# Casting q to fp16 in DRAM as 18 x 8 blocks of 4 KB instead of one contiguous stretch

## The chip, the cores and the metric

The kernel runs on one core of one Trainium2 chip. The metric is the device time of one execution in microseconds (us). The kernel before took 274.94 us, the median of 3 runs (274.41 to 275.86).

## The reference

Eight batches, eight heads, a sequence of 576 and a head dimension of 64. A Performer attention with 128 random features is followed by an MLP mixer over tokens and channels.

```python
def _attn_ref(q, k, v, omega):
    q_s, k_s = (q * scale, k * scale)
    def phi(x):                                   # random features, 128 per token
        proj = np.einsum('bhsd,md->bhsm', x, omega)
        h = proj - np.sum(x * x, axis=-1, keepdims=True) / 2.0
        h = h - np.max(h, axis=-1, keepdims=True)
        return np.exp(h) / np.sqrt(m)
    q_p, k_p = (phi(q_s), phi(k_s))
    kv = np.einsum('bhsm,bhsd->bhmd', k_p, v)
    z = np.sum(k_p, axis=2)
    num = np.einsum('bhsm,bhmd->bhsd', q_p, kv)
    den = np.einsum('bhsm,bhm->bhs', q_p, z)[..., None] + 1e-06
    return num / den

def _moe_ref(x, w_tok1, w_tok2, w_ch1, w_ch2):    # x: batch, 576, 8 heads * 64
    xt = x.transpose(0, 2, 1)
    h = np.maximum(xt @ w_tok1, 0.0) @ w_tok2     # 576 -> 256 -> 576
    u = x + h.transpose(0, 2, 1)
    h2 = np.maximum(u @ w_ch1, 0.0) @ w_ch2       # 512 -> 1536 -> 512
    return u + h2
```

## The kernel before, in words

**Stages of a batch.** The program works batch by batch, with neighbouring batches overlapped. For batch b: the features of k (matmuls at L571 for the last 64 tokens and at L679 for the first 512, exponentials at L534) and of q (L641 and L691, L534); k's features times v (L735, with v scaled on GpSimd at L315 just before); the attention's numerators and denominators (L768); the token mixing (L796, L803, then L816, L870); a transposition of u by a DMA (L824) into the tile uT; the channel mixing, whose first product reads uT (L1144, from batch 5 on L1073) and whose second product is L1178 or L961.

**How q and k reach the core.** The feature matmuls need q and k with the head dimension on the partitions, in fp16. Batches 0 and 1 are transposed on TensorE. For batches 2 to 7, the function `load_transposed` (L375) does it in two DMA steps. GpSimd issues casting DMAs from fp32 in DRAM to fp16 in a DRAM scratch (`q16_b`, `k16_b`): for q one DMA for all 576 tokens (`cast`, L379); for k one for the first 512 tokens (`cast_main`, L384) and two for the last 64 (`cast_tail`, L390). Then SyncE issues a transposing DMA from the scratch into the tile qT or kT (`back`, L400), which waits for the landing of its casts. A row of the scratch holds 128 fp16 elements, so q's scratch of a batch is 2304 rows, 589,824 bytes.

**What sets the order.** Nothing is decided at run time: `Planner.run` (L154) issues the jobs by a written list of numbers (`ORDER`, L22). So the instructions of each engine stand in a fixed row, and each waits for the semaphores of what it needs. Two queues matter here. GpSimd (POOL in the profile) issues all casting DMAs and the loads of v, between its own multiplications. SyncE (SP) issues the transposing DMAs of q, k and u and some of the stores; a wait at its head holds up all that stands behind it. All DMAs that GpSimd issues go into the one software queue, q0 of the profile.

The rows of SyncE around the first two transposed batches are these (kT and qT of batch 2, then uT of batch 1, then two stores, then qT and kT of batch 3):

```order
L400 DMA_TRANSPOSE kT_89<-k_2_152 128x1x2304
L400 DMA_TRANSPOSE qT_86<-q_2_151 128x1x2304
L824 DMA_TRANSPOSE uT_127<-u_123 128x16x128
L1188 DMA out_dram<-o_132 128x512
L1188 DMA out_dram<-o_131 128x512
L400 DMA_TRANSPOSE qT_84<-q_3_153 128x1x2304
L400 DMA_TRANSPOSE kT_87<-k_3_154 128x1x2304
```

Thus a late cast of batch 2 also holds the transposition of u of batch 1, and a late cast of q of batch 3 holds kT of the same batch.

Of the kernel before, what the change touches and what calls it, by code (L numbers as in the profile page):

```python
# [137 lines left out]
class Planner:  # L138
# [38 lines left out]
    def place(self, tag, name):  # L177
        return self.held[tag, name]
# [7 lines left out]
def kernel(  # L186
# [14 lines left out]
    B, H, S, D = q.shape  # L201
# [4 lines left out]
    P = 128  # L206
# [7 lines left out]
    R = SM // 2  # L214
# [84 lines left out]
    scratch = {}  # L299
# [3 lines left out]
    src = {"q": q, "k": k}  # L303
# [26 lines left out]
    def dma(eng, key, wire, fn, deps=(), take=(), give=(), cost=None):  # L330
        cost = (0.75 if eng == "POOL" else 0.45) if cost is None else cost
        job = add(eng, cost, key, fn, deps, take, give, wire=wire)
        return job
# [41 lines left out]
    def load_transposed(b, key, deps=()):  # L375
        casts = {"q": [], "k": []}
        for n, w in enumerate("qk"):
            def cast(w=w):
                nc.gpsimd.dma_start(  # L379
                    out=scratch[w, b].rearrange("(p r) e -> p (r e)", p=P),  # L380
                    in_=src[w][b].rearrange("h s d -> (h s d)").rearrange("(p f) -> p f", p=P),
                )
            def cast_main(w=w):
                nc.gpsimd.dma_start(  # L384
                    out=scratch[w, b][0 : H * R].rearrange("(h c r) e -> c h (r e)", h=H, c=P // H),
                    in_=src[w][b, :, 0:SM, :].rearrange("h s d -> h (s d)").rearrange("h (c f) -> c h f", c=P // H),
                )
            def cast_tail(w=w):
                for g in range(2):
                    nc.gpsimd.dma_start(  # L390
                        out=scratch[w, b][H * R : H * RA, g * D : (g + 1) * D],
                        in_=src[w][b, 4 * g : 4 * g + 4, SM:S, :],
                    )
            if w == "k":
                casts[w].append(dma("POOL", key + 0.01 * n - 0.005, 0.8, cast_tail, deps, cost=1.1))
            casts[w].append(dma("POOL", key + 0.01 * n, 3.2, cast if w == "q" else cast_main, deps, cost=0.55))
        for n, w in enumerate("qk"):
            def back(w=w):
                t = (t_qT if w == "q" else t_kT)[place(w + "T", b)]
                nc.sync.dma_start_transpose(out=t.unsqueeze(1), in_=scratch[w, b])  # L400
            ld[w + "T", b] = dma("SP", key + 0.2 + 0.01 * n, 2.2, back, deps=casts[w], take=[(w + "T", b)], cost=2.5)
# [25 lines left out]
    def clear(t):  # L427
# [6 lines left out]
        out=w1m.rearrange("p j t -> p (j t)"), in_=moe_w_tok1[0:SM, :].rearrange("(p j) t -> p (j t)", j=NJ)))  # L434
# [23 lines left out]
    for i in range(2):  # L458
        c0 = i * (NCB // 2)
        j_wc2.append(dma("POOL", -3.0 + 0.1 * i, 3.85, lambda c0=c0: nc.gpsimd.dma_start(  # L460
            out=wc2[:, c0 : c0 + NCB // 2, :], in_=moe_w_ch2[c0 * P : (c0 + NCB // 2) * P, :].rearrange("(i p) d -> p i d", p=P))))
# [5 lines left out]
    for out_, a, b in ((T1, W12, W11), (T2, W22, T1), (T3, W22, W12), (T4, W21, T2)):  # L467
# [3 lines left out]
        out=omega16.rearrange("p (i d) -> p i d", i=2), in0=omega_nat.unsqueeze(1).broadcast_to((P, 2, D)), scalar1=c_scale, scalar2=None, op0=ALU.mult), deps=j_om)  # L471
# [779 lines left out]
```

## Time and profile before

| what | value |
| --- | --- |
| median of the runs | 274.94 us (274.41 to 275.86, 3 runs) |
| the profiled execution, its own time | 273.79 us |
| its span, from the first to the last instruction | 272.0 us |
| TensorE (PE) busy | 262.9 us, 97% of the span |
| VectorE (DVE) busy | 227.2 us, 84% |
| ScalarE (ACT) busy | 164.2 us, 60% |
| GpSimd (POOL) busy | 134.6 us, 49% |
| granted TensorE clock, mean | 0.998 |
| casts of q (L379) | 6 DMAs, 576 KB each in the profile's count, median 7.6 us from issue to landing |
| casts of k, first 512 tokens (L384) | 6 DMAs, 512 KB each, median 7.1 us |

Times in the views are microseconds from the start of the span. A DMA's landing is counted from the start of the instruction that issues it. In the rows of the DMA queues stand packets, megabytes, and the time that the packets took as a share of 16 DMA engines over the window; the share can pass 100%, since packets on one engine overlap. The page's bytes of a packet are those written.

### The profile page before, as it was taken

Reading aid. Unit: us, or ns where it says so; the run is one execution under the profiler, and the core shown is the slowest. Engines: PE = TensorE matmul, PEld = TensorE weight load, DVE = VectorE, ACT = ScalarE, POOL = GpSimd, SP = SyncE. Lnnn points to the kernel's source line nnn. Section 1 sums busy time; section 2 is a strip of 40 time slices with the busy share of each in tenths; the row PEclk is TensorE's granted clock in tenths of the full one; section 3 lists DMA queues with packets and bytes.
Section 4 is the critical chain, followed back from the end, with each engine's and each line's share of the span. In section 5 each row is a group of like instructions: output and inputs, shape, how many; then the busy total and the mean of one; then the engine's idle time right before and its main releaser. Section 6 shows DMA issues by size and latency. Waiting matters only on the chain.

```text
span 272.0 us, 6648 instructions
## 1 busy us (share of the span) xinstructions
PE 262.9 (97%) x2647; PEld 180.0 (66%) x2647; DVE 227.2 (84%) x479; ACT 164.2 (60%) x361; POOL 134.6 (49%) x146
## 2 busy tenths in 40 slices
PE   7799999999999999999999999999999999999992
PEld 4367455444568655766578546986789688888881
DVE  3897879876998799987889799899997795799992
ACT  2999941188695338736746865699947541573500
POOL 8895492064803490079459996964145044600001
PEclk9999999999999999999999999999999999999999
DMA  8999999999999999989989986980260063030134
GB/s 199 190 208 210 191 210 185 216 202 132 180 204 156 223 187 175 164 160 158 171 178 173 194 233 64 182 167 2 49 128 2 23 193 58 0 157 0 63 133 119
DMA packets 81296, 39.70 MB, mean 146 GB/s; under 512 B 63984, under 2 KB 77040, under 8 KB 81072
## 3 DMA queue, kind: packets, MB, share of 16 engines
q0 software_dynamic: 31744, 17.74, 44.2%
q1 hardware_dynamic: 46928, 15.37, 29.5%
q10 hardware_dynamic: 2592, 6.16, 6.4%
q8 instruction: 20, 0.33, 0.5%
q14 instruction: 12, 0.10, 0.1%
HBM read 35.95 MB, written 16.52 MB: 193 GB/s over the span
## 4 chain that ended last, share of the span: by engine, by line
PE 86%; DMA 8%; POOL 3%; DVE 1%; issue 0%; POOLq 0%; SPq 0%
PE bank L961 24%; PE bank L1144 19%; PE bank L1073 13%; PE bank L803 5%; PE bank L816 5%; DMA uT<-u 4%; DMA w1m<-in_moe_w_tok_dram 4%; PE bank L1178 4%; PE bank L679 3%; PE bank L768 3%; PE bank L735 3%; PE bank L691 2%; POOL r L339 1%; PE bank L870 1%; PE bank L842 1%; PE bank L854 1%
## 5 line engine op out<-in xcount | busy, mean ns | idle before, releaser
L1144 PE MATMUL bank<-uT,wc 128*128 128x512 f16 x232 | 56.0, 379 | 0.0
L315 POOL TENSOR_TENSOR vs<-v,vs 128x512 f16<-128x512 f16 x31 | 33.1, 1072 | 42.8 <-DVE vs L716 33.5
L310 ACT ACTIVATE r<-bank 128x512 f16<-128x512 f32 (+1 forms) x61 | 34.5, 598 | 26.5 <-PE bank L1144 16.0
L961 PEld LDWEIGHTS <-r 128*128 128x128 f16 x384 | 36.7, 98 | 7.2 <-issue 1.6
L534 ACT ACTIVATE kp<-bank 128x512 f16<-128x512 f32 x64 | 35.5, 623 | 9.6 <-PE bank L679 8.9
L712 DVE TENSOR_REDUCE km<-kp 128x8 f16<-128x1024 f16 x32 | 38.5, 1204 | 2.0 <-ACT kp L534 2.0
L534 ACT ACTIVATE qp<-bank 128x512 f16<-128x512 f32 x64 | 36.5, 620 | 4.3 <-PE bank L691 4.3
L1144 PEld LDWEIGHTS <-wc 128*128 128x128 f16 x232 | 20.5, 98 | 20.1 <-issue 1.1
L961 PEld LDWEIGHTS <-S 128*128 128x128 f16 x288 | 27.7, 98 | 4.7 <-issue 0.4
L786 DVE TENSOR_TENSOR x<-bank,rc 128x320 f16<-128x320 f32 x53 | 25.2, 483 | 1.1
L941 DVE TENSOR_TENSOR o<-u,bank 128x512 f32<-128x512 f16 x28 | 19.1, 680 | 5.8 <-PE bank L961 5.3
L961 PE MATMUL bank<-T,r 128*128 128x256 f16 x192 | 23.8, 273 | 0.0
L961 PE MATMUL bank<-T,S 128*128 128x256 f16 x192 | 23.4, 272 | 0.0
L961 PE MATMUL bank<-wc,r 128*128 128x256 f16 x192 | 23.1, 273 | 0.0
L312 DVE TENSOR_SCALAR r<-bank 128x512 f16<-128x512 f32 (+1 forms) x29 | 18.9, 661 | 3.1 <-PE bank L1144 2.4
L819 DVE TENSOR_TENSOR u<-x,bank 128x512 f16<-128x512 f16 x28 | 17.9, 681 | 1.9 <-PE bank L816 1.9
L315 POOL TENSOR_TENSOR vbd<-vt,vbd 128x512 f16<-128x512 f16 x6 | 6.4, 1060 | 23.5 <-DVE vbd L616 18.5
L768 PEld LDWEIGHTS <-qp 128*128 128x128 f16 x256 | 14.0, 98 | 5.9 <-issue 0.3
L1073 PE MATMUL bank<-uT,wc 128*128 128x256 f16 x120 | 16.6, 273 | 0.6 <-DMA uT<-u 0.6
L941 DVE TENSOR_TENSOR o<-o,bank 128x512 f32<-128x512 f32 x21 | 14.3, 680 | 3.1 <-PE bank L961 2.9
L775 DVE RECIPROCAL rc<-bank 128x5 f32<-128x5 f32 x64 | 11.2, 184 | 6.7 <-PE bank L770 3.7
L768 PE MATMUL bank<-kvsb,qp 128*128 128x65 f16 x256 | 16.0, 193 | 0.2 <-ACT qp L534 0.2
(151 smaller groups left out, 551.3 us busy)
## 6 DMA issues: line engine op xcount, KB each, us to landing
out_dram<-o ACTq DMA_DIRECT2D x9, 512.0 KB, 3.7
q<-in_q_dram POOLq DMA_DIRECT2D x6, 576.0 KB, 7.6
wc<-in_moe_w_ch_dram POOLq DMA_DIRECT2D x4, 768.0 KB, 11.1
k<-in_k_dram POOLq DMA_DIRECT2D x6, 512.0 KB, 7.1
v<-in_v_dram POOLq DMA_DIRECT2D x6, 512.0 KB, 8.6
out_dram<-o SPq DMA_DIRECT2D x5, 512.0 KB, 3.1
r<-in_q_dram POOLq DMA_DIRECT2D x4, 288.0 KB, 7.1
v<-in_v_dram POOLq DMA_DIRECT2D x4, 256.0 KB, 8.9
```

Of the source, the lines that this page charges most:

```text
L310: nc.scalar.activation(out=out, in_=in_, func=AF.Relu)
L312: nc.vector.tensor_relu(out=out, in_=in_)
L315: (nc.gpsimd if eng == "POOL" else nc.vector).tensor_tensor(**kw)
L534: nc.scalar.activation(out=out, in_=in_, func=AF.Exp, bias=0.0, scale=1.0)
L712: nc.vector.reduce_max(out=t_km[place("km", (b, hp))], in_=src_, axis=AX.X)
L768: nc.tensor.matmul(ps[:, k, j * 65 : (j + 1) * 65], st, s[:, i, 0 : D + 1], start=True, stop=True)
L786: nc.vector.tensor_tensor(out=to, in0=ps, in1=rc.unsqueeze(2).broadcast_to((P, NJ + 1, D)), op=ALU.mult)
L819: nc.vector.tensor_tensor(out=t_u[place("u", b)][:, j, :], in0=t_x[place("x", b)][:, j, :], in1=bank(n), op=ALU.add)
L941: nc.vector.tensor_tensor(out=o, in0=a, in1=ps, op=ALU.add)
L961: nc.tensor.matmul(ps[:, j * DH : (j + 1) * DH], a[:, cb, j * P : (j + 1) * P], w[:, cb, :], start=(bank_of(b, j0) not in held and j == j0 ...
L1073: nc.tensor.matmul(ps[:, n, :], w(a)[:, (2 * m + n) * P : (2 * m + n + 1) * P], x_[:, a], start=(what in ("P1", "P2", "P5") and n == 0 and ...
L1144: nc.tensor.matmul(ps, wc1[:, db, cb * P : (cb + 1) * P], moving(db), start=(db == 0), stop=(db == ND - 1))
```

## The change

One DMA form is changed, the cast of q at L379, issued six times (batches 2 to 7).

```diff
             def cast(w=w):
                 nc.gpsimd.dma_start(
-                    out=scratch[w, b].rearrange("(p r) e -> p (r e)", p=P),
-                    in_=src[w][b].rearrange("h s d -> (h s d)").rearrange("(p f) -> p f", p=P),
+                    out=scratch[w, b].rearrange("(h c r) e -> c h (r e)", h=H, c=S * D // (R * 8)),
+                    in_=src[w][b].rearrange("h s d -> h (s d)").rearrange("h (c f) -> c h f", c=S * D // (R * 8)),
                 )
```

With S = 576, D = 64 and R = 256, c is 18: a head's 36,864 elements are cut into 18 blocks of 2048 elements (8 KB read, 4 KB written). The blocks are walked with the block number outside and the head inside, 18 times 8 pieces. Source and destination of every element stay as they were. Before, the whole is contiguous, and the program as built holds it as 32 pieces of 9216 elements (18,432 bytes written). The form of the k cast at L384 is 16 times 8 pieces of 2048 elements in both kernels.

On GpSimd, the place of the first two changed DMAs shows that the form alone is different, and the neighbours keep their order:

```order
 L371 DMA vt_93<-in_v_dram 64x4x64
 L315 TENSOR_TENSOR vs_106<-v_91,vs_106 128x8x64
-L379 DMA q_2_151<-in_q_dram 32x9216
+L379 DMA q_2_151<-in_q_dram 18x8x2048
 L390 DMA k_2_152<-in_k_dram 256x1x64 x2
 L357 DMA v_92<-in_v_dram 128x8x256
 L315 TENSOR_TENSOR vbd_113<-vt_93,vbd_113 128x8x64
-L379 DMA q_3_153<-in_q_dram 32x9216
+L379 DMA q_3_153<-in_q_dram 18x8x2048
 L390 DMA k_3_154<-in_k_dram 256x1x64 x2
 L384 DMA k_3_154<-in_k_dram 16x8x2048
```

The rows of TensorE, VectorE, ScalarE and SyncE are the same in both programs.

## The prediction

> **What bounds the kernel now.** I read the page's busy times first, then the busy time by stage, then the waits. The page's row of the engines:
>
> ```profile
> PE 262.9 (97%) x2647; PEld 180.0 (66%) x2647; DVE 227.2 (84%) x479; ACT 164.2 (60%) x361; POOL 134.6 (49%) x146
> ```
>
> The busy time by stage, in two stages in which casts of q are issued (window, its length, then busy time and instructions of PE, PEld, DVE, ACT and POOL, granted clock, DMA share, GB/s):
>
> ```profile
> 40.00:60.00 20.00, 20.00 (x180) 10.46 (x180) 16.55 (x33) 7.65 (x17) 5.51 (x7) 1.00 1.15 186
> 60.00:80.00 20.00, 20.00 (x185) 10.56 (x182) 16.79 (x39) 15.90 (x32) 9.45 (x12) 1.00 1.21 187
> ```
>
> TensorE is busy for 20.00 of 20.00 us in each, at full clock: it bounds the kernel and does not wait for a DMA there. In the view of waits, the only matmuls behind the start-up that wait for a DMA are these two, and the chain of waits has them at 200 and 228 us:
>
> ```profile
> PE bank L1073 <- DMA uT<-u: 0.6, 2, 0.3
> ```
> ```profile
> 194.41 6.04 DMA uT<-u
> 222.46 5.85 DMA uT<-u
> ```
>
> The last cast of q is issued at 152.1 us (the row of L379 below).
>
> Two consequences. A quicker DMA can win nothing in the stages where q is cast. A slower one costs exactly what it overruns its slack by, and since TensorE has no idle time to catch up with, such a delay stays to the end. So the question is the slack of q's casts, and how much longer each takes.
>
> **The change, part by part: one cast.** What a piece costs comes from two stretches in which the software queue carries pieces of one size alone. First pieces of the q cast of batch 4 (window 77.12 to 78.5 us), the totals and the queue's row:
>
> ```profile
> DMA packets 16, 0.29 MB, mean 214 GB/s; under 512 B 0, under 2 KB 0, under 8 KB 0
> q0 software_dynamic: 16, 0.29, 99.9%
> ```
>
> 16 pieces of 18,432 bytes (0.29 MB) took 99.9% of 16 engines for 1.38 us: 1.38 us each. Then the k cast of batch 4 in pieces of 4096 bytes (window 90.05 to 92.6 us):
>
> ```profile
> q0 software_dynamic: 142, 0.52, 102.4%
> ```
>
> 0.52 MB are 128 pieces of 4096 bytes (the other 14 packets are a few bytes each): 102.4% of 16 engines for 2.55 us, 41.8 us in all, 0.326 us each. By the byte a small piece is 6% dearer.
>
> Before, 32 pieces on 16 engines are 2 each: 2.76 us per engine. Now there are 144 pieces. If they were dealt out singly, 9 per engine, it would be 2.93 us, 0.17 us more. But the DMA's outer count is now 18, and the outer blocks hold 8 pieces each. If an engine takes whole outer blocks, 18 blocks on 16 engines leave at least one engine with two, 16 pieces: 5.22 us, **2.46 us more** than before. No DMA of the kernel before has an outer count that isn't a multiple of 16 (the k cast's 16 blocks give one to each engine), so no row shows which it is. Bounds: 0.17 and 2.46 us per cast, longer under contention (below). I take 2.46: the nearest row is the k cast, whose 16 blocks can be given out whole, and nothing in this trace ever needed a cut inside an outer block.
>
> The Trainium skill, "DMA: Bandwidth & Descriptors", section "Why a DMA increments its semaphore by 16 and not by 1", has a rule against this change: a DMA uses the largest number of engines up to 16 that divides the outermost counts of both sides, which for 18 is 9, two blocks on each. No run here shows it yet. By it the fullest engine has the same 16 pieces, so the sum below would be the same, with all nine equally full.
>
> GpSimd's time to issue a cast of q and one of k (ns, least, median, most), and the page's rows of their landing:
>
> ```profile
> L379 POOL DMA_DIRECT2D q<-in_q_dram x6: 533/555/582, 39.4 to 152.1; - x6
> ```
> ```profile
> L384 POOL DMA_DIRECT2D k<-in_k_dram x6: 557/574/601, 36.1 to 147.4; - x6
> ```
> ```profile
> q<-in_q_dram POOLq DMA_DIRECT2D x6, 576.0 KB, 7.6
> k<-in_k_dram POOLq DMA_DIRECT2D x6, 512.0 KB, 7.1
> ```
>
> The smaller pieces cost GpSimd 0.02 us a cast, which its idle half hides. Some engines get less to do than before; nothing waits for that.
>
> **The first cast on the path: batch 2.** GpSimd's row of the two k tails (right behind q in its queue; the second starts half way, at 40.8), SyncE's rows (start, duration), then the landings from issue of the second tail, of kT and of uT of batch 1, then the matmuls that need kT and uT:
>
> ```profile
> 39.97 1.70 POOL L390 DMA_DIRECT2D k<-in_k_dram  x2
> ```
>
> ```profile
> 47.81 2.71 SPq L400 DMA_TRANSPOSE kT<-k  x1
> 50.57 2.34 SPq L400 DMA_TRANSPOSE qT<-q  x1
> 54.30 1.73 SPq L824 DMA_TRANSPOSE uT<-u  x1
> ```
> ```profile
> DMA to landing us min/median/max: 6.9/6.9/6.9
> DMA to landing us min/median/max: 5.0/5.0/5.0
> DMA to landing us min/median/max: 5.6/5.6/5.6
> ```
> ```profile
> 54.84 0.29 PE L571 MATMUL bank<-omT,kT 64*128 64x128 f16 x4
> 60.50 0.82 PE L1144 MATMUL bank<-uT,wc 128*128 128x512 f16 x3
> ```
>
> The k tail lands at 47.7 us, and kT starts at once: it is released by the DMA that stands behind q's cast in the same queue. With the fullest engine 2.46 us late, kT starts at 50.3 and lands at 55.3, where L571 starts at 54.84: a wait of about 0.4 us. Its cover until now was 2.0 us. qT then starts at 53.0 and holds SyncE until 55.4, so uT goes out 1.1 us late and lands at 61.0 instead of 59.9; the first L1144, moved to 60.9, waits another 0.1. Sum **0.5 us**.
>
> **The second: batch 3.** GpSimd's rows, SyncE's rows and its wait, then the landings of q's cast, of qT and of kT, and the matmuls that use these:
>
> ```profile
> 57.07 1.05 POOL L315 TENSOR_TENSOR vbd<-vt,vbd 128x512 f16<-128x512 f16 x1 [14.49 <-DVE vbd L616]
> 58.07 0.58 POOL L379 DMA_DIRECT2D q<-in_q_dram  x1
> ```
> ```profile
> 66.27 3.30 SPq L400 DMA_TRANSPOSE qT<-q  x1
> 69.75 3.20 SPq L400 DMA_TRANSPOSE kT<-k  x1
> ```
> ```profile
> SPq L400 <- DMA q<-in_q_dram: 7.6, 1, 7.6
> ```
> ```profile
> DMA to landing us min/median/max: 8.1/8.1/8.1
> DMA to landing us min/median/max: 6.8/6.8/6.8
> DMA to landing us min/median/max: 7.5/7.5/7.5
> ```
> ```profile
> 74.03 0.28 PE L641 MATMUL bank<-qT,omT 64*128 64x256 f16 x2
> 78.05 0.61 PE L679 MATMUL bank<-omT,kT 64*128 64x128 f16 x16
> ```
>
> SyncE waits 7.6 us for this very cast, which lands at 66.2, and sends qT at 66.27. qT lands at 73.1, 0.9 us ahead of L641. Late by 2.46, it lands at 75.5: a wait of 1.5 us. kT is sent right behind, now at 72.2, and lands at 79.7; L679, moved by 1.5 to 79.55, waits 0.2. Sum **1.7 us**. It adds to batch 2's, since the cast is issued behind vbd, which waits on work that follows batch 2's L571 and so moves with TensorE.
>
> **The other four casts.** Of these, batch 6 has the least slack. Its cast, the cast's landing and qT:
>
> ```profile
> 128.20 0.53 POOL L379 DMA_DIRECT2D q<-in_q_dram  x1
> ```
> ```profile
> DMA to landing us min/median/max: 10.4/10.4/10.4
> ```
> ```profile
> 144.03 4.14 SPq L400 DMA_TRANSPOSE qT<-q  x1
> ```
>
> 128.20 + 10.4 is 138.6, 5.4 us before qT is sent. I take nothing for these four. One by-effect is left open: batch 6's cast runs into kT of that batch, whose row, landing and user are
>
> ```profile
> 135.63 5.13 SPq L400 DMA_TRANSPOSE kT<-k  x1
> ```
> ```profile
> DMA to landing us min/median/max: 7.5/7.5/7.5
> ```
> ```profile
> 144.59 0.28 PE L571 MATMUL bank<-omT,kT 64*128 64x128 f16 x4
> ```
>
> It lands at 143.1, 1.5 us early. An overrun of the cast hits it by 0 to 2.46 us: 0 to 1.0 us of waiting. I take 0, since the cast's last pieces and the transposition share engines only in part, and keep 1.0 for the range.
>
> **Sum.** 0.5 + 1.7 = 2.2 us. On the profiled execution, 273.79 becomes 276.0. Its own time lies 1.15 below the median of the runs, so for the median I add the same 2.2: **277.1 us**, 0.8% slower.
>
> **Rivals.** *Dealt out evenly, and transpositions gain (not slower).* With 9 pieces per engine a cast ends 0.17 us later, under the 0.9 us of the tightest slack; and a transposition's packets stand behind pieces of 0.326 instead of 1.38 us. The point from which it decides: 2.76 + 0.9 us is 11 pieces on the fullest engine; up to there nothing waits. The skill's same page, section "SWDGE vs HWDGE vs iDMA", speaks for it: a DMA engine changes between queues at the ends of packets of preferably 4096 bytes or less; the rows above show packets of 18 KB before the change. But TensorE has no wait for DMA to give back there, so this wins nothing: 274.9, within 274.4 to 275.6.
>
> *Whole blocks, but the full engines aren't the late ones.* The cast of batch 4 landed in
>
> ```profile
> DMA to landing us min/median/max: 7.0/7.0/7.0
> ```
>
> so 8.1 for batch 3 holds 1.1 us of disturbance on some engines. If those aren't the ones with 16 pieces, the cast lands at 7.0 + 2.46, 1.4 us late: 0.5 us at L641, perhaps 0.2 more at kT, and nothing at batch 2. 275.6, from 275.0 to 276.1.
>
> *Contention multiplies it.* In the window 60.6 to 63.1, batch 3's pieces
>
> ```profile
> q0 software_dynamic: 30, 0.55, 135.1%
> ```
>
> took 135.1% of 16 engines for 2.5 us, 1.80 us each, 1.31 times the quiet 1.38. Then 16 pieces are 6.8 us against 3.6: 3.2 us late, 2.5 us of waiting at batch 3, with 0.5 at batch 2 and 1.0 at batch 6: 278.9.
>
> **How the numbers follow.** My forecast (277.1, from 276.0 to 277.9) has 0.45; even dealing 0.23; full engines not late 0.17; contention 0.15. The range takes in all four: 274.4 to 279.0, leaving out about 0.1. A measurement of this kernel can tell about 0.5% (1.4 us) from no change, so slower begins at 276.3. Slower: 0.39 of the forecast's 0.45, all 0.15 of the contention, 0.04 of the others: 0.58. Faster, 0.05, lies in even dealing alone, if the unprofiled runs, which are 1.15 us above the profiled one, hold waits for transpositions that this trace doesn't show. The same: 0.37.
>
> **What would show it.** The landing of q's casts should rise by about 2.5 us from its median of 7.6, with the k tails behind them; the k casts at L384 that don't stand behind q should stay near 7.1. SyncE should wait over 9 us for q of batch 3 and send qT some 10.6 us after the cast's issue instead of 8.2. TensorE should have waits at L641 with qT as releaser, and smaller ones at L571 or L1144. If q's landing stays below 8.5 us, the dealing is even and I am wrong. If it rises and TensorE still has no wait, a slack was larger than these rows show. If the time falls, TensorE was waiting for DMAs in a way that its busy row hides.

## The result, and the profile after

The changed kernel is slower: 1.0112 times the kernel before, with an interval of 1.0085 to 1.0139. On 274.97 us (median of six executions of the kernel before) that is 278.05, about 3.1 us more. The executions behind the ratio took 277.29, 277.88 and 278.23 us; three others (282.87, 287.45, 290.25) had a mean granted clock of 0.979 to 0.991 against 0.996 to 1.0, are left out of the ratio, and have no trace that would show why. The profiled execution took 277.29 us, span 275.5, against 273.79 and 272.0 before: 3.5 us more. The working of the prediction used profiled times, so the points below are told on that pair.

The page's row of the engines shows the same work in a longer span; the share of TensorE (PE) falls from 97% to 96%:

```profile
PE 263.5 (96%) x2647; PEld 179.9 (65%) x2647; DVE 227.8 (83%) x479; ACT 164.5 (60%) x361; POOL 135.3 (49%) x146
```

By stage (window, length, busy time and instructions of PE, PEld, DVE, ACT, POOL, clock, DMA share, GB/s), TensorE is still full at 40 to 60 us, where batch 2 is fetched, and has lost 1.22 and 0.61 us in the two stages behind it, at full clock:

```profile
40.00:60.00 20.00, 20.00 (x178) 10.61 (x178) 16.53 (x34) 7.16 (x16) 5.63 (x7) 1.00 1.14 172
60.00:80.00 20.00, 18.78 (x166) 9.46 (x162) 16.23 (x36) 14.93 (x30) 10.13 (x13) 1.00 1.16 184
80.00:100.00 20.00, 19.39 (x200) 13.34 (x201) 15.55 (x30) 9.75 (x21) 7.41 (x9) 1.00 0.91 170
```

The casts of q: GpSimd's time to issue one (ns, least, median, most), and the page's rows of landing, with k's first-512 casts beside them as a control:

```profile
L379 POOL DMA_DIRECT2D q<-in_q_dram x6: 637/699/710, 39.9 to 155.6; - x6
```
```profile
q<-in_q_dram POOLq DMA_DIRECT2D x6, 576.0 KB, 10.1
k<-in_k_dram POOLq DMA_DIRECT2D x6, 512.0 KB, 7.2
```

q's median landing rises by 2.5 us (7.6 to 10.1) and k's stays (7.1 to 7.2); the two casts of k that stand shortly behind one of q's in the queue do land later (batch 3 10.7 us after its issue instead of 9.2, batch 5 12.6 instead of 9.0). The increments of the semaphore of batch 3's cast of q, in us from its issue, one for each of the 16 engines, say how the blocks were given out (worked out from the trace's semaphore records):

```
before  5.8 5.8 5.8 5.9 5.9 6.3 6.3 | 6.4 6.4 6.6 6.7 6.8 6.9 7.0 8.1 8.1
after   3.6 3.7 3.8 3.8 3.8 3.9 4.0 | 9.2 9.2 9.2 9.2 9.2 9.2 9.3 9.3 9.3
```

Seven engines report some 5 us early, nine late: nine engines carry the data, two blocks of eight pieces each. This bears out the rule that the prediction drew from the Trainium skill, "DMA: Bandwidth & Descriptors", section "Why a DMA increments its semaphore by 16 and not by 1": the largest divisor of 18 up to 16.

SyncE's rows (start, duration) from batch 2 to batch 3, its wait for q, and the landing of kT of batch 3 from its issue:

```profile
49.81 2.68 SPq L400 DMA_TRANSPOSE kT<-k  x1
52.54 2.48 SPq L400 DMA_TRANSPOSE qT<-q  x1
55.06 2.05 SPq L824 DMA_TRANSPOSE uT<-u  x1
...
67.96 3.75 SPq L400 DMA_TRANSPOSE qT<-q  x1
71.89 4.16 SPq L400 DMA_TRANSPOSE kT<-k  x1
```
```profile
SPq L400 <- DMA q<-in_q_dram: 8.7, 1, 8.7
```
```profile
DMA to landing us min/median/max: 8.7/8.7/8.7
```

Every one of these five is sent later than before, by 0.8 to 2.1 us. kT of batch 3 also takes longer, 8.7 us instead of 7.5. Two windows of the queues (packets, megabytes, share) show where. From 74.1 to 78.1 us SyncE's queue, q1, moves kT's data (2304 packets of 256 bytes), and GpSimd's queue, q0, has only small pieces of other loads; from 78.31 to 80.3 us batch 4's cast of q is under way in q0, and of kT there are only 32 packets of 4 bytes, which come between its data and its landing:

```profile
q1 hardware_dynamic: 2300, 0.59, 94.0%
q0 software_dynamic: 1612, 0.05, 36.4%
```
```profile
q0 software_dynamic: 808, 0.39, 130.5%
q1 hardware_dynamic: 32, 0.00, 2.2%
```

kT's data are through 6.4 us after its issue (5.1 before; 1.0 of the 1.3 us pass ahead of their first packet), and the landing follows 2.3 us behind (2.4 before). So the extra lies in the data, ahead of batch 4's cast.

What TensorE pays is in its rows at three places (the bracket has the idle time ahead of the row and what ended it):

```profile
75.51 0.28 PE L641 MATMUL bank<-qT,omT 64*128 64x256 f16 x2 [0.92 <-DMA qT<-q]
...
80.61 0.62 PE L679 MATMUL bank<-omT,kT 64*128 64x128 f16 x16 [0.92 <-DMA kT<-k]
```
```profile
120.83 1.47 PE L1144 MATMUL bank<-uT,wc 128*128 128x512 f16 x6 [0.63 <-DMA uT<-u]
```

0.92 + 0.92 + 0.63 is 2.47 us. A further 0.57 us lies at 21 us, a wait for a weight load in the start-up, ahead of the first cast of q, and so no effect of it in this trace:

```profile
21.05 0.40 PE L842 MATMUL bank<-x,w1m 128*128 128x128 f16 x4 [0.57 <-DMA w1m<-in_moe_w_tok_dram]
```

Together that is 3.04 of the 3.5 us; the rest lies in no wait long enough to name.

### The profile page after: what moved, and what is told of

The parts are those of the page before. It is cut to its first block, busy times and chain, and to the rows that moved or that the text cites. A ratio compares the mean times of both kernels' runs of the same rounds, so it can differ in the third digit from the quotient of the medians.

```text
span 275.5 us, 6648 instructions
## 1 busy us (share of the span) xinstructions
PE 263.5 (96%) x2647; PEld 179.9 (65%) x2647; DVE 227.8 (83%) x479; ACT 164.5 (60%) x361; POOL 135.3 (49%) x146
## 4 chain that ended last, share of the span: by engine, by line
PE 77%; DMA 12%; DVE 5%; POOL 3%; issue 1%; POOLq 0%; SPq 0%
PE bank L961 22%; PE bank L1144 16%; PE bank L1073 14%; DMA uT<-u 5%; DMA w1m<-in_moe_w_tok_dram 4%; PE bank L1178 4%; PE bank L816 4%; PE bank L803 3%; DMA kT<-k 3%; PE bank L735 2%; PE bank L679 2%; PE bank L768 2%; PE bank L691 2%; DVE x L786 1%; POOL r L339 1%; DVE S L315 1%
## 5 line engine op out<-in xcount | busy, mean ns | idle before, releaser
L1144 PE MATMUL bank<-uT,wc 128*128 128x512 f16 x232 | 56.0, 379 | 0.6 <-DMA uT<-u 0.6
L961 PEld LDWEIGHTS <-r 128*128 128x128 f16 x384 | 36.7, 98 | 7.1 <-issue 1.6
L1144 PEld LDWEIGHTS <-wc 128*128 128x128 f16 x232 | 20.4, 97 | 21.2 <-DMA uT<-u 1.1
L961 PEld LDWEIGHTS <-S 128*128 128x128 f16 x288 | 27.7, 98 | 4.7 <-issue 0.4
L941 DVE TENSOR_TENSOR o<-u,bank 128x512 f32<-128x512 f16 x28 | 19.1, 682 | 5.8 <-PE bank L961 4.1
L961 PE MATMUL bank<-T,r 128*128 128x256 f16 x192 | 23.8, 273 | 0.0
L961 PE MATMUL bank<-T,S 128*128 128x256 f16 x192 | 23.4, 273 | 0.0
L961 PE MATMUL bank<-wc,r 128*128 128x256 f16 x192 | 23.1, 273 | 0.0
L775 DVE RECIPROCAL rc<-bank 128x5 f32<-128x5 f32 x64 | 11.2, 184 | 7.2 <-PE bank L770 4.3
L941 DVE TENSOR_TENSOR o<-o,bank 128x512 f32<-128x512 f32 x21 | 14.3, 681 | 3.1 <-PE bank L961 2.9
L996 POOL DMA_DIRECT2D out_dram<-x x2 | 1.3, 647 | 30.5 <-DVE x L941 30.5
## 6 DMA issues: line engine op xcount, KB each, us to landing
q<-in_q_dram POOLq DMA_DIRECT2D x6, 576.0 KB, 10.1
wc<-in_moe_w_ch_dram POOLq DMA_DIRECT2D x4, 768.0 KB, 10.7
```

The costliest lines, as they stand in the source:

```text
L941: nc.vector.tensor_tensor(out=o, in0=a, in1=ps, op=ALU.add)
L961: nc.tensor.matmul(ps[:, j * DH : (j + 1) * DH], a[:, cb, j * P : (j + 1) * P], w[:, cb, :], start=(bank_of(b, j0) not in held and j == j0 ...
L1144: nc.tensor.matmul(ps, wc1[:, db, cb * P : (cb + 1) * P], moving(db), start=(db == 0), stop=(db == ND - 1))
```

## The experiments

The theory: the cost is the number of engines that a cast of q is spread over, which makes it land late, and the lateness reaches TensorE through the transpositions of batches 2 and 3. The rivals: the small pieces themselves cost (more packets, more work for GpSimd); or the time comes from another batch, or from contention and not from the cast's own lateness. Each ratio is to the kernel before on the same chip.

### Same 4 KB pieces, all 16 engines

```diff
-                    out=scratch[w, b].rearrange("(p r) e -> p (r e)", p=P),
-                    in_=src[w][b].rearrange("h s d -> (h s d)").rearrange("(p f) -> p f", p=P),
+                    out=scratch[w, b].rearrange("(i c r) e -> c i (r e)", c=16, i=9),
+                    in_=src[w][b].rearrange("h s d -> (h s d)").rearrange("(i c f) -> c i f", c=16, i=9),
```

> All six casts of q in 144 pieces of 4 KB as in the change, but 16 outer blocks of 9 pieces instead of 18 of 8. Theory (whole outer blocks go to an engine, the fullest one sets the landing): 9 pieces of 0.326 us on each of 16 engines, 2.93 us against 2.76 before, so the casts land within 0.5 us of before (median 7.6), no wait at L641 for batch 3, and the time is that of before within 0.3% (ratio 0.997 to 1.003). Rival (small or strided pieces are slow by themselves): landings near the 10.1 us of the change, and a ratio near 1.011.

Measured: 0.9994 (0.9976 to 1.0013). The landing of q's casts, and TensorE's two rows in which the change has its waits:

```profile
DMA to landing us min/median/max: 6.7/7.5/9.5
```
```profile
74.29 0.28 PE L641 MATMUL bank<-qT,omT 64*128 64x256 f16 x2
...
78.31 0.61 PE L679 MATMUL bank<-omT,kT 64*128 64x128 f16 x16
```

The same 144 pieces, with 16 outer blocks in place of 18, cost nothing: neither row has a bracket. The small pieces are acquitted. Nor does a quicker transposition win anything (kT of batch 3 landed 7.0 us after issue, 7.5 before): TensorE had no wait for it.

### Twelve engines, in two ways

The same edit with `c=12, i=12`, and with `c=72, i=2`: both have 144 pieces of 4 KB, and 12 is the largest divisor of either outer count up to 16. Were blocks rounded up over 16 engines, 72 would use 15 of them.

```diff
+                    out=scratch[w, b].rearrange("(i c r) e -> c i (r e)", c=12, i=12),
+                    in_=src[w][b].rearrange("h s d -> (h s d)").rearrange("(i c f) -> c i f", c=12, i=12),
```

> All six casts of q in 144 pieces of 4 KB, 12 outer blocks of 12 pieces. Theory: 12 engines with 12 pieces each, 3.91 us, 1.15 us more than before: landing near 8.8 us, 0.2 to 0.5 us of waiting in batch 3 and little elsewhere: ratio 1.001 to 1.005. Rival (pieces): as the change, 1.011. Rival (number of engines has nothing to do with it): 1.00.

```diff
+                    out=scratch[w, b].rearrange("(i c r) e -> c i (r e)", c=72, i=2),
+                    in_=src[w][b].rearrange("h s d -> (h s d)").rearrange("(i c f) -> c i f", c=72, i=2),
```

> All six casts of q in 144 pieces of 4 KB, 72 outer blocks of 2 pieces. By whole blocks spread over all 16 engines, the fullest has five blocks, 10 pieces, 3.26 us, 0.5 us more than before: landing near 8.1 us, ratio 1.000 to 1.002. By the Trainium skill's rule (the largest number of engines up to 16 that divides the outer count), 12 engines with 6 blocks, 12 pieces, as in the run with 12 outer blocks: landing near 9.2 us, ratio near 1.012.

Measured: 1.0126 (1.0083 to 1.0168) for 12 x 12, more than I expected, and 1.0062 (1.0037 to 1.0086) for 72 x 2. In both, four engines report early and twelve late. Landing of q's casts, first 12 x 12, then 72 x 2:

```profile
DMA to landing us min/median/max: 7.8/9.2/10.5
```
```profile
DMA to landing us min/median/max: 7.6/8.3/10.9
```

12 x 12 lands 1.6 us later than before, about two thirds of the change's 2.5, and yet costs as much. Its trace shows where: almost nothing at L641, but a long wait at L679.

```profile
80.44 0.62 PE L679 MATMUL bank<-omT,kT 64*128 64x128 f16 x16 [1.79 <-DMA kT<-k]
```

So the wait for kT isn't proportional to the cast's lateness. 72 x 2 lands at 8.3 us, nearer to the 8.1 expected for 16 engines than to the 9.2 for twelve; it is the increments that tell the two apart. With it, on as many engines as 12 x 12, the cast lands 0.9 us earlier, no wait for kT or qT of batch 3 is left, and half the loss remains in the timed runs; why the order of the blocks matters that much wasn't tried.

### Nine engines, big pieces

9 outer blocks of 4 pieces of 16 KB: the same nine engines and the same bytes on each as the change.

```diff
+                    out=scratch[w, b].rearrange("(i c r) e -> c i (r e)", c=9, i=4),
+                    in_=src[w][b].rearrange("h s d -> (h s d)").rearrange("(i c f) -> c i f", c=9, i=4),
```

> All six casts of q in 36 pieces of 16 KB (8192 elements), 9 outer blocks of 4 pieces. Theory: nine engines carry 4 pieces of 1.38 x 16384 / 18432 = 1.23 us each, 4.9 us against 2.76, so the casts land about 2.2 us late, near 9.8 us, and the time is nearly that of the change: ratio 1.007 to 1.012. Rival (small pieces are what costs): these pieces are nearly as large as before, landing near 7.6 us and a ratio of 1.00.

Measured: 1.0294 (1.026 to 1.0328), far above what I expected. The cast lands no later than the change's, but kT of batch 3 takes 11.2 us from issue to landing in place of 8.7 (first the six casts of q, then kT):

```profile
DMA to landing us min/median/max: 9.4/9.7/11.3
```
```profile
DMA to landing us min/median/max: 11.2/11.2/11.2
```

TensorE waits, and then works at a lower clock (its row, then the stage behind it):

```profile
83.77 0.40 PE L679 MATMUL bank<-omT,kT 64*128 64x128 f16 x8 [3.33 <-DMA kT<-k]
```
```profile
84.00:88.00 4.00, 4.00 (x29) 2.17 (x23) 2.06 (x3) 2.55 (x5) 0.00 (x0) 0.60 0.71 138
```

In the same trace it waits 1.43 us at L641 for qT of batch 3, and later 1.23 us at L961 for VectorE. Two things that the prediction didn't have: a transposition stands behind big pieces of another cast that shares its engines, and a long wait is paid twice, by itself and in the clock behind it.

### The change for batch 3 alone

```diff
+                    out=scratch[w, b].rearrange("(h c r) e -> c h (r e)", h=H, c=18) if b == 3 else scratch[w, b].rearrange("(p r) e -> p (r e)", p=P),
...
```

> The new form for batch 3 alone, the five other casts as before. Theory of the prediction (batch 3 is where the time goes): the waits at L641 and L679 of batch 3 stay as in the change, 0.9 us each, and the later wait at L1144 near 120 us goes: 1.5 to 2.1 us in all, ratio 1.006 to 1.008. Rival (the loss is spread over all casts, through the queue's total time): a sixth of 3.1 us, ratio 1.002.

Measured: 1.0197 (1.0159 to 1.0235), 5.4 us: more than with all six changed. qT has no wait; kT has a long one, and the clock follows (TensorE's rows, then the stage):

```profile
74.16 0.28 PE L641 MATMUL bank<-qT,omT 64*128 64x256 f16 x2
...
81.16 1.04 PE L679 MATMUL bank<-omT,kT 64*128 64x128 f16 x16 [2.81 <-DMA kT<-k]
```
```profile
80.00:84.00 4.00, 2.85 (x21) 1.51 (x22) 0.69 (x1) 2.20 (x5) 0.00 (x0) 0.58 1.15 197
```

Batch 4's cast is here still in 32 pieces of 18,432 bytes. The queues in the window 77.5 to 80.7 us (packets, megabytes, share):

```profile
q0 software_dynamic: 602, 0.63, 108.3%
q1 hardware_dynamic: 32, 0.00, 1.4%
```

The 32 pieces (0.59 of the 0.63 MB) fill the engines, and SyncE's queue, q1, moves 32 packets of 4 bytes: kT's data are through by then, only these last packets are not, and they come out at 78.9 to 80.7. kT lands 10.7 us after its issue, with its data through at 77.0. It was sent 2.9 us ahead of batch 4's cast (70.43 and 73.31), whose issue doesn't move with SyncE. Where it was sent 3.4 to 3.5 us ahead of a cast in big pieces, before and in the kernel with batches 2, 5, 6 and 7 changed (71.86 and 75.29), it landed after 7.5 and 7.2 us. So half a microsecond seems to decide; that margin wasn't tried by itself.

Batch 4's cast is only part of it. Worked out from the packet records of each trace, kT of batch 3 spends its time so (us; the last row is the next experiment):

| kernel | kT sent at | its data through, from its issue | from there to its landing |
| --- | --- | --- | --- |
| before | 69.75 | 5.1 | 2.4 |
| 16 x 9 | 69.92 | 4.8 | 2.2 |
| 72 x 2 | 70.45 | 5.9 | 2.1 |
| 12 x 12 | 71.00 | 7.1 | 2.3 |
| the change | 71.89 | 6.4 | 2.3 |
| 9 x 4, big pieces | 72.48 | 7.4 | 3.8 |
| batch 3 alone | 70.43 | 6.6 | 4.1 |
| batch 3, batch 4 in small pieces | 71.73 | 6.7 | 3.0 |

With batch 3's cast on nine or twelve engines the data take 0.8 to 2.3 us longer; what slows them wasn't tried. The last part grows by 1.4 to 1.7 us where a late kT meets a cast of batch 4 in big pieces, by 0.6 with small ones on 16 engines, and not at all in the change itself.

### Batch 3 changed, batch 4 in small pieces on 16 engines

```diff
+                    out=scratch[w, b].rearrange("(h c r) e -> c h (r e)", h=H, c=18) if b == 3 else scratch[w, b].rearrange("(i c r) e -> c i (r e)", c=16, i=9) if b == 4 else scratch[w, b].rearrange("(p r) e -> p (r e)", p=P),
...
```

> Batch 3's cast in the new form, batch 4's in 144 pieces of 4 KB on 16 outer blocks, the others as before. New theory: with batch 3 late, kT's transposition ends when batch 4's cast starts, and its completion is held behind that cast's pieces on every engine; with 18 KB pieces (the run with batch 3 alone) for over 3 us, long enough that the granted clock halves for 3.4 us. With 4 KB pieces it is held for about 1.5: kT lands 8.5 to 9.5 us after its issue instead of 10.7, L679 waits 1.0 to 1.8 us instead of 2.8, the clock stays at 1.0, ratio 1.004 to 1.008 instead of 1.020. Rival (the prediction's: only the lateness of q's cast counts, batch 4's pieces don't matter): as with batch 3 alone, 2.8 us of waiting and 1.02.

Measured: 1.0144 (1.0121 to 1.0166), below batch 3 alone, above what I expected. TensorE's row and the stage around it:

```profile
81.45 0.62 PE L679 MATMUL bank<-omT,kT 64*128 64x128 f16 x16 [1.81 <-DMA kT<-k]
```
```profile
80.00:84.00 4.00, 2.55 (x29) 1.76 (x30) 1.77 (x5) 2.44 (x6) 0.00 (x0) 1.00 1.23 198
```

With small pieces behind it, kT takes 9.7 us instead of 10.7 although it was sent 1.3 us later (the difference is in the last part, 3.0 against 4.1), the wait falls from 2.81 to 1.81, and the clock stays whole. So batch 4's big pieces are part of what batch 3 alone costs, and the halved clock another.

### The other batches

The form of the change for all but batch 3, for batch 5, for batch 4, and for batches 2, 5, 6 and 7. The conditions in place of `b == 3`:

```diff
+ ... if b != 3 else ...
```

> The new form for batches 2, 4, 5, 6 and 7, the old one for batch 3. Theory (batch 3's late cast is the cause of most of the loss): no wait at L641 and L679 of batch 3, what is left is 0 to 0.7 us at L1144 near 118 us: ratio 1.000 to 1.004. Rival (every cast on nine engines costs its share): five sixths of the change's 1.1%, ratio 1.009.

```diff
+ ... if b == 5 else ...
```

> The new form for batch 5 alone. Theory: the 0.6 us wait at L1144 near 120 us in the changed kernel comes from batch 5's cast, whose pieces on nine engines (and the k casts behind them) run into the transposition of u of batch 3; alone it gives 0 to 0.6 us: ratio 1.000 to 1.003, and the transposition lands later than the 6.4 us of before. Rival (that wait is a consequence of batch 3's delay only): no wait, the transposition as before.

```diff
+ ... if b == 4 else ...
```

> The new form for batch 4 alone. New theory: the load of v for batch 3 stands right behind this cast in the queue and lands near 87 us instead of 82.8, where GpSimd's first multiplication of batch 3 needs it at 86.2; the wait goes on to L735 and shows in most executions: ratio 1.003 to 1.012. Theory of the prediction (qT of batch 4 has over 5 us of slack, so this cast costs nothing): ratio 0.999 to 1.001.

```diff
+ ... if b not in (3, 4) else ...
```

> The new form for batches 2, 5, 6 and 7, the old one for 3 and 4. Both theories: batch 2 gives 0 to 0.5 us at kT and at u's transposition, the others nothing: ratio 1.000 to 1.003. Rival (all casts share the loss evenly): four sixths of 1.1%, 1.007.

Measured: batch 5 alone 1.0006 (0.9987 to 1.0024) and batch 4 alone 1.0008 (0.9984 to 1.0031), nothing, as the prediction had it. The theories of these two runs themselves fell. With batch 5 alone, the transposition of u of batch 3 lands after 6.5 us, as before (6.4), and L1144 has no wait; with batch 3 alone it lands after 6.3, and there is none either, so neither of the two alone gives the 0.63 us of the change. With batch 4 alone, v of batch 3 does land at 87.2 us, but no matmul waits for it. But all except batch 3 is 1.014 (1.0108 to 1.0171) and batches 2, 5, 6, 7 are 1.0107 (1.0066 to 1.0147), where I expected at most 1.004 and 1.003. My theory that batch 3 carries nearly all of it fell. TensorE's rows with batches 2, 5, 6 and 7:

```profile
56.38 0.29 PE L571 MATMUL bank<-omT,kT 64*128 64x128 f16 x4 [0.81 <-DMA kT<-k]
...
62.55 0.82 PE L1144 MATMUL bank<-uT,wc 128*128 128x512 f16 x3 [0.44 <-DMA uT<-u]
```
```profile
117.67 1.47 PE L961 MATMUL bank<-T,r 128*128 128x256 f16 x12 [0.69 <-DVE o L941]
```

The first two are the predicted chain of batch 2 (kT held by the k tail behind q's cast, then uT behind qT), at 1.25 us in place of 0.5; kT took 6.1 us to land here, 5.0 before. The third is something new: VectorE's L941 was itself late, and had waited for a store of o:

```profile
DVE o L941 <- DMA out_dram<-o: 1.1, 1, 1.1
```

### Stores behind the late engines

With all but batch 3 changed, v of batch 3 landed at 87.3 us, behind batch 4's cast, where it was 82.8 before. To see whether that is the cost, v's load goes ahead of the cast:

```diff
-    402, 650, 312, 383, 323, 384, 385, 418, 419, 380, 317, 324, 649, 381, 382, 506, 514, 327, 520, 515, 437, 440,
+    402, 650, 312, 383, 323, 384, 385, 418, 419, 380, 317, 324, 381, 382, 506, 649, 514, 327, 520, 515, 437, 440,
```

> As the run with all batches but 3 in the new form (ratio 1.014), with one change of order on GpSimd: the load of v for batch 3 is issued just ahead of batch 4's cast instead of just behind it. New theory (v behind the cast is where that run loses): v lands near 82 us, no wait of GpSimd for it, ratio 1.000 to 1.006. Rival (the cast delays something else, such as the transposition of q or k): 1.014 stays.

Measured: 1.0193 (1.0159 to 1.0227), slower yet; the theory that v is the cost fell. But its trace shows the path of a store in the clear. VectorE's row, TensorE's row, and the stage behind them:

```profile
87.37 0.69 DVE L941 TENSOR_TENSOR o<-u,bank 128x512 f32<-128x512 f16 x1 [3.95 <-DMA out_dram<-o]
```
```profile
88.11 2.29 PE L961 MATMUL bank<-T,r 128*128 128x256 f16 x10 [2.67 <-DVE o L941]
```
```profile
88.00:92.00 4.00, 3.89 (x25) 2.42 (x25) 3.83 (x8) 0.23 (x1) 2.35 (x3) 0.57 0.89 174
```

The semaphore increments of batch 4's cast (issued at 74.39) and of the store of o (issued at 78.94 from ScalarE's queue), us from the issue of each:

```
cast    6.2 6.2 6.2 6.2 6.3 6.3 6.3 | 11.1 11.2 11.4 11.5 12.6 12.6 12.6 12.7 12.8
store   2.2 2.2 2.2 2.2 2.3 2.3 2.3 | 7.0 7.0 8.0 8.1 8.1 8.2 8.3 8.3 8.3
```

The store is done after 2.3 us on seven engines, and on nine it ends with the cast (85.9 to 87.2 us, the cast 85.5 to 87.2). It lands with the last of the 16, so nine loaded engines delay a store that has nothing to do with q. The store behind the wait at 117.67 us above is split the same way (2.5 to 2.6 us on seven, 5.2 to 6.8 on nine), and so is one in the change itself, sent at 81.28 us (1.8 to 2.0 and 4.9 to 5.4); there VectorE waits 1.0 us for it and TensorE doesn't. For a transposition such a split isn't shown in the change: kT of batch 3 has its 16 increments within 0.6 us. The end of the store frees the buffer that VectorE writes next, and TensorE waits for VectorE.

### Work in the wait

To test the clock, 8 matmuls of 512 columns were to stand ahead of L679 in the kernel with batch 3 alone, and break up the wait:

```diff
-                ps = [bank((n_k, e)) for e in range(2)]
+                ps = [bank((n_k, e)) for e in range(2)]; [nc.tensor.matmul(ps[0], wc1[:, 0, 0:P], wc1[:, 0, 0:SM], start=True, stop=True) for _ in range(8 if n_k[1:] == (3, 0) else 0)]
```

> As the run with batch 3 alone in the new form (ratio 1.0197), with 8 idle matmuls of 512 columns (1.7 us, their results overwritten) put on TensorE ahead of the L679 that waits for kT of batch 3. Theory (the 2.8 us wait halves the granted clock for 3.4 us, which costs 1.7 us on top): the wait shrinks to 1.1 us, the clock stays at 1.00, and in spite of the added work the time falls by 1 to 1.7 us, ratio 1.013 to 1.016. Rival (the clock has nothing to do with the wait): the ratio stays at 1.02, since the added matmuls only fill idle time.

Measured: 1.0261 (1.0211 to 1.0312). The job that they hang on comes 11.5 us behind the wait, so they broke up nothing (the wait, then the eight):

```profile
82.12 1.03 PE L679 MATMUL bank<-omT,kT 64*128 64x128 f16 x16 [3.29 <-DMA kT<-k]
...
93.65 1.90 PE L673 MATMUL bank<-wc 128*128 128x512 f16 x8
```

Eight matmuls some 0.21 us apart are 1.7 us, 0.6%, and 1.0197 + 0.006 is what was measured, though its trace also has the lower clock for twice as long as that of batch 3 alone (last section), so the close match is partly luck. The run says nothing on whether a filled wait keeps the clock.

## Why the prediction held, and where it did not

The forecast of 2.2 us stands against a measured 3.1 (2.3 to 3.8 by the interval). 278.05 us lies above the forecast's own 276.0 to 277.9 and inside the range for all four possibilities, 274.4 to 279.0. The main mechanism is shown: whole outer blocks on fewer engines, a later landing, waits of TensorE that it can't make good. That the sum came near is in part luck: the places that it names have 1.84 us of waiting in the trace, none of it at batch 2, and 0.63 us lie at one that it doesn't name. Term by term:

- **What bounds the kernel** held. TensorE was full before; every wait that a late DMA made came out as time, and with 16 engines (16 x 9) nothing was gained.
- **One cast, +2.46 us**: the median landing rose by 2.5. Nine engines, as the rule said. Cast by cast it is 0.6 (batch 6) to 3.6 us (batches 5 and 7), and 1.8 and 1.2 for batches 2 and 3, the two in the sum; the agreement of the median is partly luck.
- **GpSimd's 0.02 us** for issuing was wrong: 0.70 us instead of 0.56, seven times the estimate taken from the k cast. 16 x 9 costs it 0.60 and 72 x 2 0.76. Its idle time covers it.
- **Batch 2, 0.5 us**: no wait in the changed kernel's trace. kT was sent at 49.81 instead of the 50.3 that I worked out and landed at 54.9, and L571, 0.5 us late from the start-up, stood at 55.33. With batches 2, 5, 6 and 7 the same chain cost 1.25. The place was right, and it costs from nothing to over 1 us, by what else has delayed TensorE.
- **Batch 3, qT 1.5 us**: 0.92. qT landed at 75.5 us, just where the working had it, but because errors cancelled: the cast was issued 0.5 us later (58.57), after the start-up's wait, and landed 9.3 us after its issue, not 10.6; then qT took 7.5 us, not 6.8. The wait is shorter because L641 itself stood some 0.5 us later. The 8.1 of before holds about 1.1 us of disturbance that did not come on top of the 16 pieces. That was the rival "whole blocks, but the full engines aren't the late ones", whose 9.46 was nearer; SyncE sent qT 9.4 us after the cast's issue.
- **Batch 3, kT 0.2 us**: 0.92, and 1.79 to 3.33 in the variants. This is the step that failed. I had moved kT's landing by as much as its issue and kept its 7.5 us; it took 8.7, since a later kT meets other traffic. In the change this isn't batch 4's cast: the 1.2 us lie in kT's data, which were through at 78.3 us, while that cast's first piece went out at 78.1. What slowed the data stays open; batch 4's cast lengthens the last part only in the variants with big pieces. That is contention as the third rival had it, but on the transposition and not on the cast. Nor is kT simply "sent right behind" qT: in all 14 traces it goes out 0.29 to 0.33 us after the landing of k's own first-512 cast (71.58 us here, 69.45 before), which stands behind q's cast in GpSimd's queue.
- **The other four casts, nothing**: batches 4 and 5 alone do cost nothing. But the 0.63 us at L1144 was not foreseen, nor that casts hold up stores of o. uT of batch 3 went out with TensorE, 2.7 us later than before, and took 7.7 us instead of 6.4; neither batch 3 nor batch 5 alone reproduces it, and what it met stays open.
- **Even dealing**, the rival on the other side, is what 16 x 9 built, and it came out within 0.1% of before, as worked out.

The parts don't add: batch 3 alone 5.4 us, all but batch 3 3.8, batches 2, 5, 6 and 7 2.9, all six 3.1. Two reasons are shown: batch 4's big pieces behind kT (10.7 against 9.7 us), and a clock that halved after the longest waits. How much each makes stays open, since each kernel has one trace: the trace of all but batch 3 (276.46 us) lies 2 us below the other executions behind its ratio (278.61 to 279.08), and what those wait for isn't in it. A single trace also has waits of this size that the change doesn't explain: with batch 5 alone, TensorE waits 0.79 us for kT of batch 7, whose cast of q is the old one.

## What to carry to other kernels

Give a DMA an outer count with 16 as a divisor; look at its semaphore's increments for an early and a late group to see how many engines it has. A cast on fewer engines is not only late itself: it can delay a store that is spread over all 16, and what stands behind it in its own queue. When a transposition moves, look at which other traffic it will meet, and don't keep its old duration.

## What the runs showed of the hardware

- **The clock behind a wait.** After TensorE waits of 2.67, 2.81 and 3.33 us the clock was 0.5 for 3.41 us, at most 1.7 us lost (the stretch can begin in the wait), and in the last run above (3.29) for twice that; after 1.81 and 1.79 it stayed whole. The Trainium skill, "TensorE: Matmul & The Clock Gate", section "HAM oscillation — how this bites in real kernels", gives a rule of no idle gaps over about 3.4 us; here 2.67 was enough. The length of a single wait isn't all: with batch 4 alone, the clock fell to 0.53 in a stage of the start-up, behind a longest wait of 0.86 us, while in the last run above a wait of 0.93 us in the same stretch left it whole.

```profile
11.80:15.40 3.60, 3.60 (x17) 0.84 (x13) 3.37 (x6) 2.30 (x7) 2.26 (x3) 0.53 1.19 213
```

- **The size of the pieces, seen from the neighbour.** On the same nine engines, pieces of 16 KB instead of 4 KB left the cast's landing at 9.7 against 10.1 us, but kT's at 11.2 against 8.7; 1.6 us of the difference lie between the end of kT's data and its landing (3.8 against 2.3), while batch 4's big pieces go out. There, the piece's size is paid by another queue's DMA.
